# A new written order for the first three batches of a cosine attention with a feed-forward behind it

## The chip, the cores and the metric

The kernel runs on one core of a Trainium2 chip. The metric is the device time of one execution in microseconds (us); the number quoted for a kernel is the median of its runs.

## What is computed

```python
q, k, v: (8, 12, 448, 64) float32      # batch, heads, sequence, head size
q_n = q / (norm(q, axis=-1) + 1e-06);  k_n = k / (norm(k, axis=-1) + 1e-06)
scores = q_n @ k_n.transpose(0, 1, 3, 2) / tau            # tau = 0.1
attn = exp(scores - max);  attn = attn / (sum(attn) + 1e-09)
x = (attn @ v).transpose(0, 2, 1, 3).reshape(8 * 448, 768)
h = x @ w_in                                              # (768, 2048)
out = maximum(0.01 * h, h) @ w_out                        # (2048, 768), float32
```

## The kernel before

Everything is written as **steps**. `ORDER` (lines 16 to 98) is one long string of 1,261 steps; lines 727 to 729 go through it and call, for each step, a small function that emits that step's instructions. Each engine gets its instructions in the order in which the steps stand, and runs them in that order; waits between engines follow from the tiles that a step reads and writes. So moving a step moves it on its own engine only, but it also changes which buffer or PSUM bank it gets. A step is a name and numbers: `k.3.1` is `scores(3, 1)`.

- A **slot** is one pair of heads: slots 0 to 5 are batch 0, slots 6 to 11 batch 1. From slot 12 on the data is laid out otherwise: a **unit** takes two pairs, an even slot holds its queries and the odd one behind it its keys (slots 12 and 13 are unit 0, slots 14 and 15 unit 1).
- Loads. `lq.s` loads a slot through SP's DMA queue (L219, L238 to L244, L230); slots 0 to 5 are loaded by lines 651 to 659, ahead of all steps. `lv.j` loads v for four heads (L256), `lr.b.lo.hi` the last 64 rows of v of batch b, one DMA for each of heads lo to hi (L264). `wi.0` to `wi.3` load w_in in four parts (L182): parts 0 and 1 are its columns 0 to 1023, parts 2 and 3 the others, and each part holds every other block of 128 rows, so a product with m up to 7 needs parts 0 and 1, one with m from 8 up parts 2 and 3. `wo.0`, `wo.1.0.8`, `wo.1.8` load w_out (L188), `lg.g` the v of a group of units (L282). All but `lq` are issued by GpSimd (POOL), on a queue of its own.
- Holds. `hr` (L707) and `hp.s` (L704) are tiny copies on GpSimd that wait for slot 0's data and for slot s's normalised tile, and so hold back what stands behind them on POOL. `hs.s` (L701) does the same for SP's queue.
- Norms. `sq.s.0` squares the queries of a slot, `sq.s.1` the keys, on GpSimd (L306; L300 from slot 12); `qf` and `sa` do that for slots 0 and 1 on ScalarE (ACT). `su` and `uf` sum the squares on VectorE (DVE; L319, L330), `ro` takes the root on ACT as Ln and Exp (L336, L337), `no` makes the reciprocal and multiplies on DVE (L342, L343, L359).
- Turning. `tp.s` transposes a slot on TensorE (PE) into a PSUM bank (L374); `tc` copies it out on DVE (L390), `ta` on ACT. For slot 0 this is done in two parts. From slot 12 on `tt` transposes on DVE (L400) and `td.u` spreads unit u by six DMAs on SP's queue (L409).
- Attention. `k.s.i` is the scores of key tile i (0 to 2; tile 3 is the remaining 64 keys of two slots) into two PSUM banks (L427), `x.s.i` its exponential on ACT (L438). For four heads j, `to.j` sums the exponentials (16 matmuls), `pr.j.0` and `pr.j.1` multiply them with v (16 matmuls each, L450; the last four of the 16 are those with the remaining keys), `ln.j` and `in.j` make the inverse on ACT (L462, L466), `sc.j.e` scales into `xT` on DVE (L478). For units the same is `q`, `y`, `g`, `gl`, `gi`, `gx` (L492, L500, L538, L546, L550, L564).
- Feed-forward. `f.c.m` is six matmuls of w_in's block m with chunk c of tokens (L588); with further numbers only those of the named blocks of 128 rows, so that it can begin before all heads are there. `r` is the leaky ReLU on ACT (L602). `s.c.t.lo.hi` is 16 matmuls with w_out (L624), `o` copies the result out on DVE and writes it (L640, L648).
- `w.n` is n matmuls on a constant tile: work without a use, put where PE would stand idle (L695). `tg` (L709): before it, pairs of banks are dealt from banks 0 to 3 and single banks from 4 to 7; behind it all eight are one pool. A bank is dealt in the order of the steps to the one given back longest ago.

Loaded slots from 6 on have four buffers, so `lq.10` waits for `no.6`, and so on. `hT` has one buffer: the first `r.1.m` waits for the last `s.0`. And each DMA waits for the one eight before it of its kind to land.

Of the kernel before, what the change touches and what calls it, by code (L numbers as in the profile page):

```python
# [26 lines left out]
r.0.0 f.0.1.4.5 r.0.1 f.0.2.4.5 r.0.2 f.0.3.4.5 r.0.3 no.7 lq.11 su.8.0 su.8.1 k.6.0 k.6.1 k.6.2 x.6.0 x.6.1
x.6.2 f.0.4 r.0.4 f.0.5 r.0.5 tp.7 tc.7 ro.8 no.8 hp.8 sq.10.0 sq.10.1 lv.4 wo.1.0.8 su.9.0 su.9.1 f.0.6 r.0.6
f.0.7 r.0.7 k.7.0 k.7.1 x.7.0 x.7.1 f.0.8 r.0.8 tp.8 tc.8 ro.9 no.9 hs.9 lq.12 su.10.0 su.10.1 f.0.9 r.0.9
f.0.10 r.0.10 k.7.2 k.7.3 x.7.2 x.7.3 f.0.11 r.0.11 tp.9 tc.9 ro.10 no.10 hp.10 sq.11.0 sq.11.1 wo.1.8 lv.5  # L30
# [6 lines left out]
su.15 s.0.1.384.768 o.0.1.384.768 ro.15 to.5 ln.5 in.5 pr.5.0 pr.5.1 sc.5.0 sc.5.1 s.0.2.384.768 o.0.2.384.768
no.15 tt.15 td.1 lq.19 hp.15 sq.17 su.16 q.0.0 y.0.0 q.0.1 q.0.2 y.0.1 y.0.2 f.1.0 r.1.0 f.1.1 r.1.1 f.1.2
r.1.2 ro.16 f.1.3 r.1.3 no.16 tt.16 lq.20 hp.16 sq.18 su.17 q.0.3 y.0.3 q.0.4 q.0.5 y.0.4 y.0.5 f.1.4 r.1.4
f.1.5 r.1.5 f.1.6 r.1.6 ro.17 f.1.7 r.1.7 no.17 tt.17 td.2 lq.21 hp.17 sq.19 su.18 q.0.6 y.0.6 q.1.0 q.1.1  # L40
y.1.0 y.1.1 f.1.8 r.1.8 f.1.9 r.1.9 f.1.10 r.1.10 ro.18 f.1.11 r.1.11 no.18 tt.18 lq.22 sq.20 su.19 q.1.2
y.1.2 g.0 gl.0 q.1.3 q.1.4 y.1.3 y.1.4 gi.0 f.1.12 r.1.12 f.1.13 r.1.13 f.1.14 r.1.14 ro.19 f.1.15 r.1.15
no.19 q.1.5 y.1.5 g.0.0 gx.0.0 tt.19 td.3 lq.23 hp.19 sq.21 su.20 q.1.6 q.2.0 y.1.6 y.2.0 lg.1 ro.20
s.1.0.0.384 o.1.0.0.384 no.20 tt.20 lq.24 hp.20 sq.22 su.21 q.2.1 y.2.1 q.2.2 q.2.3 y.2.2 y.2.3 s.1.0.384.768
o.1.0.384.768 ro.21 s.1.1.0.384 o.1.1.0.384 no.21 tt.21 td.4 lq.25 sq.23 su.22 q.2.4 y.2.4 q.2.5 q.2.6 y.2.5
y.2.6 s.1.1.384.768 o.1.1.384.768 ro.22 s.1.2.0.384 o.1.2.0.384 no.22 tt.22 lq.26 hp.22 sq.24 su.23 q.3.0
y.3.0 g.1 gl.1 q.3.1 q.3.2 y.3.1 y.3.2 gi.1 ro.23 s.1.2.384.768 o.1.2.384.768 no.23 q.3.3 y.3.3 g.1.0 gx.1.0
tt.23 td.5 lq.27 hp.23 sq.25 su.24 q.3.4 q.3.5 y.3.4 y.3.5 ro.24 s.1.3.0.384 o.1.3.0.384 q.3.6 y.3.6 g.1.1
gx.1.1 q.4.0 q.4.1 y.4.0 y.4.1 lg.2 s.1.3.384.768 o.1.3.384.768 no.24 tt.24 lq.28 sq.26 su.25 q.4.2 y.4.2
q.4.3 q.4.4 y.4.3 y.4.4 f.2.0 r.2.0 f.2.1 r.2.1 f.2.2 r.2.2 f.2.3 r.2.3 f.2.4 r.2.4 ro.25 f.2.5 r.2.5 no.25  # L50
tt.25 td.6 lq.29 hp.25 sq.27 su.26 q.4.5 y.4.5 q.4.6 q.5.0 y.4.6 y.5.0 f.2.6 r.2.6 f.2.7 r.2.7 f.2.8 r.2.8
# [713 lines left out]
```

## Time and profile before

| | us |
|---|---|
| median of three runs (414.4 to 415.75) | 415.35 |
| the profiled execution: its time, its span | 415.95, 414.0 |
| TensorE busy, of the span | 403.3 |
| VectorE, ScalarE, GpSimd busy | 261.5, 247.3, 113.6 |
| mean granted clock of TensorE | 1.000 |
| `w.20` ends | 7.50 |
| first score product (`k.0.0`), first exponential (`x.0.0`) | 9.62, 10.03 |
| end of the multiply of slot 3 (`no.3`) | 20.73 |
| w_in parts 0, 1 have landed | 24.2, 30.5 |
| first product with w_in (`f.0.0.0.2`) | 31.40 |
| transposes of slot 6 (`tp.6`) | 36.92 |
| w_in part 3 and w_out's first half have landed | 42.0, 53.4 |
| `pr.3.0`, the first product with batch 1's v | 59.62 |
| first scores of unit 0 and unit 1 (`q.0.0`, `q.1.0`) | 81.60, 93.75 |

In the timeline views a row is a run of like instructions on one engine: its start in the span, how long it took from first start to last end, engine, line, operation, tiles, how many, and in brackets how long the engine had been idle before it and what ended that. An end on PE is that of the last matmul with its way through the array; the next matmul starts some 0.15 us before it.

### The profile page before, as it was taken

How to read it: one execution, taken by the hardware profiler on the slowest of the kernel's cores; microseconds unless marked ns; L12 is line 12 of the kernel's file. 1: busy time of each engine (PE TensorE's matmuls, PEld its weight loads, DVE VectorE, ACT ScalarE, POOL GpSimd, SP SyncE). 2: the span in 40 equal slices, each digit the busy share in tenths (PEclk: the TensorE clock that was granted, in tenths of full speed). 3: DMA queues.
4: the chain of work that ended last, by engine and by line, in shares of the span. 5: the costliest groups of instructions: out<-in, count | busy, mean ns of one | idle time of the engine just before them, and what ended most of it. 6: DMA issues, size and time to landing. Idle time of an engine off the chain costs nothing.

```text
span 414.0 us, 11078 instructions
## 1 busy us (share of the span) xinstructions
PE 403.3 (97%) x4662; PEld 211.0 (51%) x4679; DVE 261.5 (63%) x424; ACT 247.3 (60%) x431; POOL 113.6 (27%) x125
## 2 busy tenths in 40 slices
...
GB/s 184 234 203 220 218 222 201 257 166 114 62 212 193 209 112 56 181 232 98 96 136 159 178 154 165 79 206 83 2 90 78 87 40 0 2 70 7 2 114 76
DMA packets 41976, 53.81 MB, mean 130 GB/s; under 512 B 12486, under 2 KB 32326, under 8 KB 41926
## 3 DMA queue, kind: packets, MB, share of 16 engines
...
q10 hardware_dynamic: 688, 0.30, 0.2%
q14 instruction: 14, 0.11, 0.1%
...
## 4 chain that ended last, share of the span: by engine, by line
PE 83%; DMA 6%; DVE 3%; issue 2%; ACT 2%; POOL 2%; SPq 1%; POOLq 0%; DVEq 0%
PE ps L624 33%; PE ps L588 32%; PE ps L538 7%; PE ps L492 6%; DMA qk_h<-in_k_dram 3%; PE ps L450 2%; DMA vq<-in_v_dram 2%; DVE qn L359 1%; DVE ss L319 1%; ACT pe L438 1%; DMA xT<-in_q_dram 1%; PE ps L427 1%; POOL sq L306 1%; SPq L409 1%; PE ps L524 1%
## 5 line engine op out<-in xcount | busy, mean ns | idle before, releaser
L624 PE MATMUL ps<-w_out_sb,hT 128*128 128x384 bf16 (+1 forms) x912 | 151.7, 324 | 0.0
L588 PE MATMUL ps<-xT,w_in_sb 128*128 128x384 bf16 (+1 forms) x753 | 150.3, 352 | 1.0 <-issue 0.3
L500 ACT ACTIVATE pe<-ps 128x896 bf16<-128x896 f32 x126 | 109.2, 917 | 46.8 <-PE ps L492 46.6
L624 PEld LDWEIGHTS <-hT 128*128 128x128 bf16 x912 | 86.4, 98 | 64.4 <-issue 10.7
L588 PEld LDWEIGHTS <-w_in_sb 128*128 128x128 bf16 x768 | 72.9, 98 | 73.5 <-issue 9.0
L602 ACT ACTIVATE hT<-ps 128x384 bf16<-128x384 f32 (+1 forms) x128 | 65.0, 552 | 62.3 <-PE ps L588 44.1
L300 POOL TENSOR_TENSOR sq<-qk_h 128x896 f32<-128x896 f32 x36 | 62.5, 1740 | 60.1 <-DMA qk_h<-in_k_dram 33.6
L640 DVE COPY osb<-ps 128x384 f32<-128x384 f32 (+1 forms) x57 | 30.7, 544 | 76.5 <-PE ps L624 72.9
L349 DVE TENSOR_TENSOR qn<-qk_h,r 128x896 bf16<-128x896 f32 x36 | 42.7, 1186 | 1.6 <-DVE r L343 0.4
L316 DVE TENSOR_REDUCE ss<-sq 128x14 f32<-128x910 f32 x36 | 38.1, 1062 | 1.1 <-POOL sq L300 1.1
L438 ACT ACTIVATE pe<-ps 128x896 bf16<-128x896 f32 x42 | 36.0, 917 | 3.2 <-PE ps L427 3.1
L492 PE MATMUL ps<-qkT 64*32 64x448 bf16 x1008 | 36.0, 352 | 0.3 <-DVE osb L640 0.3
L508 DVE TENSOR_TENSOR shared<-shared,pe 128x896 f32<-128x896 f32 x30 | 35.6, 1218 | 0.3
L564 DVE TENSOR_TENSOR xT<-ps,rb 128x448 bf16<-128x448 f32 x32 | 18.3, 614 | 20.3 <-ACT rb L550 12.4
L400 DVE STREAM_TRANSPOSE tt<-qn 128x448 f32<-128x448 f32 x36 | 29.3, 817 | 0.7
L704 POOL CAST seen<-qn 128x1 f32<-128x1 bf16 x21 | 3.9, 185 | 92.0 <-DVE qn L349 86.0
L342 DVE TENSOR_REDUCE r<-norms 128x14 f32<-128x28 f32 x48 | 8.4, 176 | 31.1 <-ACT norms L337 30.8
L538 PE MATMUL ps<-pe,vq 64*32 64x448 bf16 x1008 | 27.0, 349 | 0.0
L492 PEld LDWEIGHTS <-qkT 64*32 64x32 bf16 x1008 | 12.6, 91 | 19.2 <-issue 15.0
L336 ACT ACTIVATE ss<-ss 128x14 f32<-128x14 f32 x48 | 10.3, 215 | 18.3 <-DVE ss L316 17.2
L282 POOL DMA_DIRECT2D vq<-in_v_dram x20 | 12.7, 639 | 26.6 <-PE ps L492 26.6
L538 PEld LDWEIGHTS <-vq 64*32 64x32 bf16 x1008 | 14.6, 93 | 8.6 <-issue 0.6
...
## 6 DMA issues: line engine op xcount, KB each, us to landing
...
```

What stands on the lines that cost most here:

```text
L300: gp.tensor_tensor(sq[:, :, :D], x, x, op=ALU.mult)
L316: nc.vector.tensor_reduce(o, sqs[s], axis=AX.X, op=ALU.add)
L349: nc.vector.tensor_tensor(qn[s].rearrange("p m d e -> p m e d"), raw[s].rearrange(f"p ({t[1:-1]} d) -> p m e d", e=n, d=D), r.rearrange(f" ...
L438: nc.scalar.activation(out=dst, in_=sc[:, :, :S], func=AF.Exp, scale=inv_tau)
L492: nc.tensor.matmul(out=sc[32 * strip : 32 * strip + 32, a, :S], lhsT=x[rows, c0 : c0 + 32], rhs=x[rows, 0:S], start=True, stop=True,)
L500: nc.scalar.activation(out=pq[u, i], in_=sc[:, :, :S], func=AF.Exp, scale=inv_tau)
L508: eng.tensor_tensor(whole[u], pq[u, 0] if i == 1 else whole[u], pq[u, i], op=ALU.add)
L538: nc.tensor.matmul(out=po[32 * strip : 32 * strip + 32, w, :S], lhsT=weights, rhs=pq[us[x if two else 0], i][rows, a, :], start=(i == 0), ...
L588: nc.tensor.matmul(out=pm[:, :n], lhsT=w_in_sb[:, kt, m * 128 : (m + 1) * 128], rhs=xT[c // 2][:, kt, c0 : c0 + n], start=(done + i == 0), ...
L602: nc.scalar.activation(out=hT[c][:, m, :n], in_=pm[:, :n], func=AF.Prelu, alpha=0.01)
L624: nc.tensor.matmul(out=po2[:, : hi - lo], lhsT=hT[c][:, m, ts * 128 : (ts + 1) * 128], rhs=w_out_sb[:, m, lo:hi], start=(m == 0), stop=(m ...
L640: nc.vector.tensor_copy(out=o[:, lo:hi], in_=bank(("s", c, ts, lo))[:, : hi - lo])
```

## The change

Only `ORDER` changes, and in it only the first 487 steps; the other 774 stand as they were. The same steps are there, each once, `w` steps included: nothing is added or left out. By engine, as the order of each engine's instructions shows:

- **PE**: `tp.0.4.7` before `tp.0.0.4`; key tiles in other sequences (`k.1.2 k.1.1 k.1.3 k.1.0`, `k.2.2 k.2.0 k.2.1`, ...); `pr.0.1` before `tp.3` and `to.0`; the first w_in products before `k.5.3` and `k.5.1`; whole blocks `f.0.m` in the order 5, 6, 4, 7, 13, 15, 11, 9, 8, 10, 14, 12 instead of 4 to 15; `tp.9` before `tp.8`; `k.6.0` and the `k.9` tiles later or earlier; `pr.3` before `tp.11`; `to.5`, `pr.5` before the second halves of `s.0`; `q.0.x` before the last of them.
- **ACT**: `ro.1` before `ta.0.0.4`; `in.0` after `x.3.3`; `ro.9` before `ro.8`; `ln.5` before `ln.4`; `ro.15` before `ro.14`.
- **DVE**: `su.1` in front of `tc.0.4.7` as before, in the other sequence; `su.2.0` before `no.1`; `no.3` before `su.4`; `no.9` before `su.8.0` and `no.8`; `no.12 no.13` before `tt.12 tt.13`; `no.15` long before `no.14`.
- **POOL**: `hr` from the first place to behind `sq.5.0`, so `sq.2` stands in front of `lr.0.0.2`; keys squared before queries in slots 3, 4, 6, 8, 9; `wi.0 wi.1` one behind the other, `wi.3` before `wi.2`; `lr.1.0.4` behind `sq.9`; `lv.5` and `lv.4` behind `wo.1.0.8`; `sq.12` before `wo.1.8`; `sq.15` before `sq.14`; `lg.0` behind `sq.20`.
- **SP**: `lq.8` before `hs.3`; `lq.15` and `td.0` before `lq.14`; `lq.18 lq.19 lq.20` before `td.1`; `lq.22 lq.23 lq.24` before `td.3`.
- `tg` moves from behind the first w_in products to ahead of `k.0.0`.

```diff
-w.20 qf.0.0.3 uf.0.0.3 qf.1.0.3 uf.1.0.3 qf.0.3.4 uf.0.3.4 ro.0 hr lr.0.0.2 sa.1.1 sa.1.0 no.0 su.1.1 lq.6
-sq.2.0 sq.2.1 lv.0 tp.0.0.4 ta.0.0.4 tp.0.4.7 su.1.0 tc.0.4.7 w.3 ro.1 k.0.0 x.0.0 k.0.1 x.0.1 w.2 no.1 su.2.0
-su.2.1 lq.7 hp.1 sq.3.0 sq.3.1 lr.0.2.4 wi.0 k.0.2 x.0.2 ro.2 tp.1 tc.1 w.2 k.1.0 x.1.0 k.1.1 x.1.1 w.2 no.2
-su.3.0 sq.4.0 sq.4.1 lv.1 wi.1 k.1.2 x.1.2 w.2 tp.2 tc.2 k.1.3 x.1.3 su.3.1 ro.3 w.2 k.2.0 x.2.0 k.2.1 x.2.1
-to.0 ln.0 in.0 su.4.0 no.3 hs.3 lq.8 sq.5.0 sq.5.1 lv.2 su.4.1 k.2.2 x.2.2 tp.3 tc.3 pr.0.0 ro.4 k.3.0 x.3.0
-k.3.1 x.3.1 pr.0.1 w.2 su.5.0 no.4 lq.9 su.5.1 sc.0.0 hp.4 sq.6.0 sq.6.1 wi.2 k.3.2 x.3.2 w.2 ro.5 tp.4 tc.4
-k.3.3 x.3.3 w.2 k.4.0 x.4.0 k.4.1 x.4.1 to.1 ln.1 in.1 no.5 sc.0.1 hp.5 sq.7.0 sq.7.1 wi.3 k.4.2 x.4.2 tp.5
-tc.5 pr.1.0 k.5.0 x.5.0 k.5.1 x.5.1 pr.1.1 sc.1.0 sc.1.1 su.6.0 su.6.1 su.7.0 su.7.1 wo.0 sq.8.0 sq.8.1 lv.3
-lr.1.0.4 k.5.2 x.5.2 f.0.0.0.2 f.0.1.0.2 k.5.3 x.5.3 f.0.0.1 f.0.1.1 f.0.0.3 f.0.1.3 tg ro.6 to.2 ln.2 in.2
...
-lq.13 f.0.12 r.0.12 k.8.0 k.8.1 k.8.2 x.8.0 x.8.1 x.8.2 f.0.13 r.0.13 tp.10 tc.10 su.11.0 su.11.1 f.0.14
-r.0.14 f.0.15 r.0.15 ro.11 k.9.0 k.9.1 k.9.2 x.9.0 x.9.1 x.9.2 no.11 hp.11 sq.12 sq.13 hs.11 lq.14 s.0.0.0.384
-o.0.0.0.384 su.12 tp.11 tc.11 to.3 ln.3 in.3 pr.3.0 pr.3.1 sc.3.0 sc.3.1 ro.12 k.10.0 k.10.1 x.10.0 x.10.1
...
+qf.0.0.3 qf.1.0.3 uf.0.0.3 qf.0.3.4 uf.1.0.3 uf.0.3.4 w.20 ro.0 no.0 sa.1.1 sq.2.0 tp.0.4.7 sq.2.1 sa.1.0
+su.1.0 su.1.1 tp.0.0.4 lr.0.0.2 lq.6 lv.0 sq.3.1 ro.1 ta.0.0.4 tc.0.4.7 sq.3.0 w.2 tg w.2 lr.0.2.4 k.0.0
+su.2.0 lv.1 sq.4.1 no.1 x.0.0 su.2.1 k.0.2 k.0.1 sq.4.0 w.2 tp.1 tc.1 x.0.1 w.3 x.0.2 ro.2 wi.0 su.3.1 wi.1
+lq.7 sq.5.0 no.2 k.1.2 w.2 k.1.1 k.1.3 k.1.0 su.3.0 x.1.2 x.1.1 x.1.0 ro.3 w.2 tp.2 tc.2 w.2 x.1.3 w.2 no.3
+k.2.2 k.2.0 k.2.1 x.2.2 x.2.1 pr.0.1 su.4.1 x.2.0 su.4.0 ro.4 tp.3 tc.3 hr hp.1 sq.5.1 su.5.0 to.0 k.3.0 ln.0
+k.3.1 k.3.2 no.4 lq.8 hp.4 lv.2 su.5.1 x.3.0 x.3.2 pr.0.0 x.3.1 w.2 tp.4 tc.4 ro.5 k.3.3 no.5 k.4.1 x.3.3 in.0
+x.4.1 wi.3 to.1 hp.5 pr.1.0 tp.5 ln.1 k.4.2 sq.6.1 sc.0.1 sc.0.0 in.1 tc.5 sc.1.0 k.4.0 pr.1.1 sq.6.0 x.4.2
+k.5.2 sc.1.1 k.5.0 x.4.0 wi.2 f.0.0.0.2 f.0.1.0.2 sq.7.0 su.6.0 x.5.2 k.5.3 x.5.0 su.6.1 ro.6 k.5.1 sq.7.1
+wo.0 x.5.1 su.7.0 x.5.3 f.0.1.3 f.0.1.1 f.0.0.3 f.0.0.1 f.0.3.0.1.2.3 f.0.2.0.1.2.3 lv.3 sq.8.1 hs.3 su.7.1
+no.6 sq.8.0 to.2 ro.7 lq.9 ln.2 pr.2.1 sq.9.1 in.2 sc.2.1 pr.2.0 tp.6 sc.2.0 f.0.5 f.0.2.4.5 r.0.2 tc.6 sq.9.0
...
+lq.12 lv.4 x.9.0 ro.11 x.8.0 s.0.0.0.384 x.8.1 no.11 lq.13 o.0.0.0.384 k.10.1 k.9.3 k.8.2 x.8.2 sq.12 pr.3.0
+pr.3.1 tp.11 tc.11 x.9.3 in.3 x.10.1 s.0.1.0.384 wo.1.8 sq.13 hp.8 su.12 sc.3.0 sc.3.1 k.11.1 k.11.2 k.11.0
+su.13 o.0.1.0.384 ro.12 x.11.1 hp.10 x.11.0 ro.13 hs.11 s.0.2.0.384 x.11.2 k.10.2 no.12 x.10.2 k.11.3 k.10.0
+no.13 tt.12 tt.13 x.10.0 to.4 x.11.3 lq.15 pr.4.1 pr.4.0 to.5 pr.5.1 pr.5.0 ln.5 hp.13 s.0.0.384.768 hp.11
+sq.15 ln.4 in.4 td.0 su.15 lq.14 sq.14 hp.12 s.0.1.384.768 o.0.2.0.384 lq.16 in.5 q.0.2 ro.15 sc.4.1 lq.17
+sc.5.1 no.15 sc.4.0 o.0.0.384.768 sq.16 sc.5.0 o.0.1.384.768 y.0.2 hp.15 q.0.1 q.0.0 su.14 tt.15 f.1.9
+s.0.2.384.768 y.0.0 y.0.1 r.1.9 f.1.13 ro.14 sq.17 su.16 o.0.2.384.768 q.0.3 q.0.5 lq.18 q.0.4 ro.16 y.0.3
+no.14 lq.19 f.1.0 f.1.5 sq.19 y.0.5 f.1.4 f.1.12 f.1.10 no.16 r.1.4 r.1.12 r.1.5 su.17 tt.14 f.1.6 f.1.15
+r.1.10 ro.17 tt.16 no.17 r.1.0 tt.17 su.19 f.1.1 lq.20 td.1 td.2 lq.21 hp.16 y.0.4 r.1.13 r.1.6 q.1.0 q.1.1
...
```

More of the change, by code (lines that the diff above doesn't have):

```diff
@@ L27 @@
[L27 to L30, printed above, removed]
-lq.13 f.0.12 r.0.12 k.8.0 k.8.1 k.8.2 x.8.0 x.8.1 x.8.2 f.0.13 r.0.13 tp.10 tc.10 su.11.0 su.11.1 f.0.14
@@ L37 @@
[L37 to L51, printed above, removed]
```

48 lines of the change are left out of this document (30 added, 18 removed).

## The prediction

> **What bounds the kernel now.** I read the busy shares first, then stretches of the span, then the timeline of each engine in the first stretch, then the DMA queues. TensorE is busy 403.3 of 414.0 us, at a granted clock of 1.00 throughout. The change adds and removes no matmul, so it can only move TensorE's idle time. Where that lies, the stretches tell (span, then busy time of PE, weight loads, DVE, ACT, POOL, clock, DMA share, GB/s):
>
> ```profile
> 0.00:31.40 31.40, 25.16 (x220) 9.86 (x222) 23.87 (x60) 24.32 (x42) 21.89 (x34) 1.00 1.02 207
> 31.40:80.00 48.60, 48.54 (x507) 26.28 (x506) 38.63 (x71) 33.77 (x68) 24.80 (x29) 1.00 1.18 221
> 350.00:414.00 64.00, 60.80 (x463) 34.13 (x464) 9.89 (x19) 12.36 (x23) 0.00 (x0) 1.00 0.13 44
> ```
>
> 6.24 us are idle before the first product with w_in at 31.40 and next to none from there to 350; the last 3.2 lie in steps that don't change. So the change wins or loses in the opening, and what it wins must survive to 130 us, where the old order resumes. The DMA share above 1 from 0 to 80 us says that the DMA engines are full there too. In the opening TensorE waits for short chains (idle time and its releaser in brackets):
>
> ```profile
> 9.62 0.55 PE L427 MATMUL ps<-qkT 64*128 64x448 bf16 x4 [0.34 <-DVE qkT L390]
> ...
> 20.32 0.81 PE L374 MATMUL ps<-id,qn 128*128 128x128 bf16 x7 [1.23 <-DVE qn L359]
> ...
> 31.40 0.82 PE L588 MATMUL ps<-xT,w_in_sb 128*128 128x384 bf16 x4
> ...
> 36.92 0.55 PE L374 MATMUL ps<-id,qn 128*128 128x128 bf16 x7
> ```
>
> The largest, 1.23 us, is `tp.3` behind `no.3`.
>
> **Part by part.** *1. The first copies.* ScalarE's timeline:
>
> ```profile
> 8.29 0.56 ACT L390 COPY qkT<-ps 128x512 bf16<-128x512 bf16 x1
> 9.34 0.22 ACT L336 ACTIVATE ss<-ss 128x14 f32<-128x14 f32 x1 [0.48 <-DVE ss L319]
> ...
> 10.03 2.54 ACT L438 ACTIVATE pe<-ps 128x896 bf16<-128x896 f32 x3 [0.23 <-PE ps L427]
> ```
>
> The copy `ta.0.0.4` used idle time ahead of `ro.1`. Now it stands behind it: `su.1.0` follows `sa.1.0` (end 8.38) and with `su.1.1` ends at 9.6, `ro.1` (0.46) at 10.1, the copy (0.56) at 10.6. `k.0.0` goes from 9.62 to 10.6, `x.0.0` from 10.03 to 11.0. Price: **1.0 us** at the head of ACT's chain. That `tp.0.4.7` goes first, and so waits until 8.28 instead of 7.82, lies under that wait.
>
> *2. Slot 3 is normalised earlier.* `su.4.0`, which waited for POOL until 18.45, stands behind `no.3` now. `hr` no longer stops POOL at the start, and `sq.3.1` needn't wait for the remaining rows, so `sq.3` ends at 14.1 instead of 15.36. `x.1` runs from 13.8 to 16.3 (three at a stride of 0.81), `su.3.0` ends at 16.2, `ro.3` at 16.7; `no.3` (1.65) starts at 16.75 instead of 19.09. What may stretch it is in VectorE's rows:
>
> ```profile
> 13.58 2.20 DVE L359 TENSOR_TENSOR qn<-xT,r 128x512 bf16<-128x512 f32 x2
> ...
> 19.57 1.16 DVE L359 TENSOR_TENSOR qn<-xT,r 128x512 bf16<-128x512 f32 x2
> ```
>
> The first row is `no.2`, beside GpSimd's squares at 13.09 to 15.36; the same two multiplies otherwise take 1.16. In the new order `no.2` is clear of squares and `no.3` lies beside `sq.4.0`, so `no.3` costs 0 to 1.04 more; I take 0.5 and end it at 18.9 (20.73 before).
>
> *3. The rest of slots 3 to 5.* `pr.0.1` now comes before `tp.3` and needs v. `lr.0.2.4` is issued at 14.0 (two squares and three DMA issues earlier than 15.31 allows) and lands 3.4 to 3.9 later, 17.9 at best; with `lr.0.0.2` and `lv.0` moved behind `sq.2`, up to 19.5. I take 18.8 for its last four matmuls. Then `tp.3` 19.3, `tc.3` 20.7 (21.80), `to.0`, `ln.0`, `x.3` from 21.4 to 23.9 (25.15), because `in.0` is moved behind `x.3.3`. `to.1` can start before `x.3.3` ends, only its last four matmuls need it. `no.5` ends at 25.7 (27.34), `sc.0` at 26.8, `in.1` at 27.2, `sc.1.0` at **27.9** (30.10). `tg` lets a score take any free pair of banks, which ends the waits of 0.2 to 0.35 on exponentials before `k`. The `w` steps fill the same gaps as before and cost nothing as long as they stand in idle time. The first w_in product is at 28.4 instead of 31.40: a head start of 3.0, less `k.5.1` (0.2), which follows later. Of it 2.8 would be left at `tp.6` if the data were there.
>
> *4. w_in and the slot loads.* It isn't all there. `wi.1` is issued at 18.6 (19.98), but `lq.8` no longer waits for `no.3`, so slots 8 and 9 are loaded from 17 and 20.5 instead of 21.6 and 24.4, beside w_in. How the queues share, two stretches show, 18 to 24 and 32 to 40 us:
>
> ```profile
> q0 software_dynamic: 844, 0.92, 105.7%
> q1 hardware_dynamic: 158, 0.05, 3.3%
> ```
>
> ```profile
> q0 software_dynamic: 696, 1.37, 90.3%
> q1 hardware_dynamic: 671, 0.37, 21.9%
> ```
>
> In the first, w_in had the engines alone; in the second, each queue sent as many packets as the other, and 671 packets of the slots took 0.219 x 8 = 1.75 us, 0.0026 each. `wi.1` landed at 30.54, with some 600 slot packets by then. In the new order GpSimd's queue holds 512 + 384 + 384 packets from `lv.1` to the end of `wi.1` (192 KB in 384 B, 768 KB in 2 KB each), so packet for packet some 1,280 slot packets pass: 680 x 0.0026 = 1.8 later; `lv.2`, now behind, takes about 0.7 off. **31.6.** Bounds: 26.2 (18.6 plus the shortest landing, 7.6) and 33.0 (all of both slots ahead). The Trainium skill ("DMA: Bandwidth & Descriptors", Queues, rings and completion order) says that a DMA engine takes turns between queues packet by packet, whatever the packets' size; the two stretches agree. A split by bytes would give `wi.1` at about 30.5.
>
> `f.0.1.3` wants `wi.1` at 29.8 and gets it at 31.6; from there four single matmuls 0.65, `f.0.3` and `f.0.2` 1.3, `to.2` 0.77, `pr.2` 1.53: `tp.6` at **35.9** instead of 36.92, 1.0 us ahead. `x.5.3` (end 32.5) is in time. Then `wi.2`, now last, lands at 42 to 43 (41.99 for the last part before) and is wanted at 43.1 (`f.0.13` stands where `f.0.8` stood, at 44.35, with one `k` less before it).
>
> *5. Batch 1.* The first product with batch 1's v is the next place without slack:
>
> ```profile
> 35.26 2.49 POOL L264 DMA_DIRECT2D shared<-in_v_dram  x4
> ```
>
> ```profile
> DMA to landing us min/median/max: 21.0/22.6/23.2
> ```
>
> These four DMAs are `lr.1.0.4` (GpSimd's timeline, and their landings). The last landed at 59.56, and the last four matmuls of `pr.3.0` began at about 60.2. They queue behind `wo.0` (landed 53.43) and `lv.3`; all that stands ahead of them is the same bytes as before, through engines that are full, and slots 12 and 13 start at about 49.4 instead of 50.09 beside them. So I keep 59.2, with bounds 56.2 (the first of the four) and 60. The new `pr.3.0` has the same work ahead of it (`tp.11` 0.4 less, two `k` more): its last four come at 60.2 - 1.0 = 59.2, just served. A larger head start would end here. `wo.0` is wanted at 55. `lv.4`, now issued at 53.4 behind `wo.1.0.8` (landed 66.0 before, with slot 14's load beside it), should land by 67 and is wanted at 68.
>
> *6. Units.* `td.0` ends on SP at 74 and lands by 76; `q.0.2` wants it at 78.9 - 1.0 = 77.9. But `lq.14` now stands behind `td.0`: issued 74, landed 78.8, `sq.14` 80.5, then on DVE `su.14`, `tt.15`, `su.16`, an output copy, `no.14`, `no.16`, `su.17`, `tt.14` (1.1 + 0.65 + 1.05 + 0.55 + 1.65 + 1.65 + 1.05 + 1.0) to 89.4, `td.1` 3.8 and 2.0 to land: 95.3. `q.1.0` has two `f` more and one `q` less ahead of it than before: 93.75 + 2.7 - 1.0 = 95.4. Just served again. `td.3`, behind `lq.24`, lands 11.2 us after `s.1.0.0.384` ends (copy 0.6, `tt` 1.65, `no.20` 1.65, `lq.24` 1.2, `td.3` 3.75, landing 2.4), and `q.3.0` comes 11.9 after it. I count nothing for both.
>
> *7. The rest:* key tiles and w_in blocks in other sequences, `ln.5` before `ln.4`, `tp.9` before `tp.8`, `lg.0` at 93 for a use at 107. Nothing, since between a score product and the first use of its exponential lie w_in blocks of 0.98 each or whole `s` of 2.6; where that cover is gone, an exponential (0.92) shows.
>
> Sum: 1.0 us won by `tp.6`, kept to the end. On the profiled execution's own time, 415.95 (414.0 span, 1.95 around it), that is 414.95; its time is 0.6 above the median, so in the measure of the runs 415.35 - 1.0, **414.3**.
>
> **The rivals.** *The opening's gain in full.* If `wi.1` lands by 30 and the remainders by 57.5, 2 to 2.7 us stay: 412.6 to 413.4. For it: 27.9 for `sc.1.0` doesn't hang on a DMA. Against it: full DMA engines and four places (`wi.1`, `pr.3.0`, `td.1`, `td.3`) with little slack.
>
> *The late first exponential is not made good: slower.* ACT is busy 24.3 of the first 31.4 us. From `x.0.0` to `x.5.3` it had 21 exponentials at 0.81, four roots at 0.46, two pairs `ln`, `in` at 1.1, 21.0 us, and took 23.5, so 2.5 idle. Now `ro.6` is among them too: 21.5 from 11.0, and with the same idle time `x.5.3` ends at 35.0, the last four matmuls of `to.2` come 1.3 later than before, and so does the end: **416.6**. It decides from 1.0 us of idle time on (11.0 + 21.5 + 1.0 = 33.5, as before); I count 0 to 1, since `ro` and `x` are now seldom late, but fills on newly dealt banks now wait for exponentials as well (`w.2` and `tp.2` for `x.1.2`).
>
> *Unit 1 is late.* Each us that slot 14's chain loses (a load landing after 10 us like slot 10's, two stretched multiplies) is one on TensorE at `q.1.0`: 2 to 4 give 416.3 to 418.3.
>
> **How the numbers follow.** The forecast, 0.3 to 1.9 won: 0.48. The full gain: 0.20. The late exponential: 0.18. Unit 1 late: 0.14. About 0.3% (1.25 us) is what a measurement of this kernel can tell from no change. The forecast puts 0.18 beyond that and 0.30 within; the full gain is faster; of the late exponential 0.04 is within, the rest and unit 1 slower: faster 0.38, same 0.34, slower 0.28. Range: from the full gain's 412.6 to the late exponential's 416.6; unit 1 is left out. The forecast's own range is 413.4 to 415.1.
>
> **What would show it.** `k.0.0` at 10.6; `no.3` ending near 18.9 and `sc.1.0` near 27.9; an idle stretch of some 1.8 us on PE before `f.0.1.3`, released by the w_in DMA; `tp.6` at 35.9; no gap at `pr.3.0` and `q.1.0`. Wrong: `x.5.3` after 33.5, a gap over 1 us at `pr.3.0` or `q.1.0`, or `wi.1` before 30.

## The result and the profile after

The changed kernel takes **417.27 us** (median of 14 runs, 415.33 to 420.19) where the kernel before takes 415.33 on the same chip (14 runs, 414.40 to 416.08): ratio **1.0051, 95% interval 1.0036 to 1.0067**. The forecast was 414.3, faster, with 416.6 as the upper end. It came out slower, and outside the range.

The profiled execution of the changed kernel took 417.69 us, with a span of 415.9. Its stretches (columns as before: span, then busy time of PE, weight loads, DVE, ACT, POOL, clock, DMA share, GB/s):

```profile
0.00:29.85 29.85, 25.77 (x217) 10.51 (x219) 24.29 (x60) 22.04 (x40) 18.83 (x31) 1.00 1.00 217
29.85:80.00 50.15, 47.99 (x526) 26.20 (x524) 39.16 (x70) 34.67 (x68) 23.69 (x28) 1.00 1.03 186
80.00:130.00 50.00, 48.46 (x564) 24.18 (x560) 34.50 (x53) 34.30 (x60) 20.89 (x21) 1.00 0.65 160
350.00:415.90 65.90, 62.69 (x474) 35.20 (x475) 9.90 (x19) 14.11 (x27) 0.00 (x0) 1.00 0.12 43
```

Idle time of PE is span less busy time. Ahead of the first product with w_in it fell from 6.24 to 4.08 us. From there to 80 us it rose from 0.06 to 2.16, and between 80 and 130 us it is 1.54 (0.21 before, by the same view). The end is as it was: 3.21. So the opening won and the two stretches behind it lost more. Idle time makes the opening look better than it is: the matmuls without a use of `w.20` happened to take 7.28 us here and 5.85 before, and that counts as busy. PE's timeline shows where (start, time, then idle time and releaser in brackets):

```profile
10.55 0.74 PE L427 MATMUL ps<-qkT 64*128 64x448 bf16 x6 [0.36 <-ACT qkT L390]
...
20.56 0.56 PE L374 MATMUL ps<-id,qn 128*128 128x128 bf16 x7
...
29.85 0.82 PE L588 MATMUL ps<-xT,w_in_sb 128*128 128x384 bf16 x4
...
32.02 2.12 PE L588 MATMUL ps<-xT,w_in_sb 128*128 128x384 bf16 x12 [0.65 <-DMA w_in_sb<-in_moe_w_in_dram]
...
36.46 0.56 PE L374 MATMUL ps<-id,qn 128*128 128x128 bf16 x7
...
57.21 0.34 PE L374 MATMUL ps<-id,qn 128*128 128x128 bf16 x3 [1.49 <-DVE qn L359]
...
87.01 0.38 PE L492 MATMUL ps<-qkT 64*32 64x448 bf16 x8 [0.90 <-DVE osb L640]
```

From the top: `k.0.0`; `tp.3`, whose wait of 1.23 us is gone; the first w_in product, 1.55 earlier than before; `f.0.1.3` behind w_in's second part; `tp.6`, 0.46 ahead of the kernel before; and then two waits that the prediction didn't have, 1.49 us at `tp.10` and 0.90 at `q.0.4`. With those, 0.46 ahead becomes, for equal work done, 1.1 behind at the first `s.0` and about 1.6 behind at `q.1.0`.

**The wait at `tp.10`.** VectorE's rows of the four normalises `no.2`, `no.3`, `no.6` and `no.10` (their two multiplies), and further down the sum `su.16` and the output copy `o.0.2.384.768`:

```profile
14.51 2.02 DVE L359 TENSOR_TENSOR qn<-xT,r 128x512 bf16<-128x512 f32 x2
...
18.15 1.16 DVE L359 TENSOR_TENSOR qn<-xT,r 128x512 bf16<-128x512 f32 x2
...
32.80 3.18 DVE L359 TENSOR_TENSOR qn<-qk_h,r 128x512 bf16<-128x512 f32 x2
...
53.98 3.17 DVE L359 TENSOR_TENSOR qn<-qk_h,r 128x512 bf16<-128x512 f32 x2
...
85.39 1.10 DVE L316 TENSOR_REDUCE ss<-sq 128x14 f32<-128x910 f32 x1 [1.60 <-POOL sq L300]
86.40 0.55 DVE L640 COPY osb<-ps 128x384 f32<-128x384 f32 x1
```

GpSimd's rows for the same times: v's load `lv.4`, slot 12's squares `sq.12`, and later slot 14's squares `sq.14`:

```profile
54.21 0.81 POOL L256 DMA_DIRECT2D shared<-in_v_dram  x1 [1.07 <-DMA w_out_sb<-in_moe_w_out_dram]
55.03 1.69 POOL L300 TENSOR_TENSOR sq<-qk_h 128x896 f32<-128x896 f32 x1
...
80.42 1.68 POOL L300 TENSOR_TENSOR sq<-qk_h 128x896 f32<-128x896 f32 x1 [7.59 <-DMA qk_h<-in_q_dram]
```

The two multiplies of a normalise take 1.16 us alone and 3.17 beside `sq.12`: 2.01 more, a little over the whole 1.69 of the square. The single records of the trace say the same: the second multiply of `no.10` runs from 54.59 to 57.15, and `sq.12` from 55.03 to 56.73; the multiply ends 0.42 after the square. In the kernel before `no.10` had 1.65 us in all, 1.16 of it the multiplies, since slot 11's squares stood behind the hold on `no.10` and slot 12's behind the hold on `no.11`. VectorE's row of `no.10` there, and GpSimd's of the two holds:

```profile
51.63 1.16 DVE L359 TENSOR_TENSOR qn<-qk_h,r 128x512 bf16<-128x512 f32 x2
```

```profile
52.92 0.18 POOL L704 CAST seen<-qn 128x1 f32<-128x1 bf16 x1 [1.25 <-DVE qn L359]
...
57.83 0.19 POOL L704 CAST seen<-qn 128x1 f32<-128x1 bf16 x1 [1.29 <-DVE qn L359]
```

The change moves both holds (`hp.10`, `hp.11`) behind slot 12's squares and loads slot 12 earlier (issued at 45.87, not 50.09). `no.6` is stretched as far, by the squares of slots 8 and 9, but `tp.6` didn't wait for it.

GpSimd's row of `lv.4`, further up, tells what set the collision. GpSimd stood still for 1.07 us, until w_out's first part had landed (53.92), because `lv.4` is the eighth DMA behind `wo.0` of its kind. `sq.12` stands behind `lv.4`, so the landing of w_out decides when it runs.

The Trainium skill ("SBUF — State Buffer", 🔬 SBUF: two separate sides) states that VectorE with two SBUF inputs and GpSimd share one pair of ports, that it is an exclusive lock for a whole instruction, and that the other one fully blocks. The 3.17 against 1.16 agrees. By its record the multiply started 0.44 us ahead of the square and was yet the one that waited, so which of the two had the pair first can't be read off the records. GpSimd was issuing `lv.4` when it started (54.21 to 55.01). That issue alone isn't what stretched it: in experiment 17 below, the same two multiplies stood beside the same issue (54.01 to 54.81), with the square held back, and took 1.16.

`no.2` is another matter. Its first multiply ran from 14.51 to 16.06, 1.55 us instead of 0.69, with no square beside it. GpSimd's rows there are squares, two issues of v's last rows, the issue of v's second tile, and squares again:

```profile
12.04 2.23 POOL L306 TENSOR_TENSOR sq<-xT 128x384 f32<-128x384 f32 x2
14.22 1.29 POOL L264 DMA_DIRECT2D shared<-in_v_dram  x2
15.51 0.79 POOL L256 DMA_DIRECT2D shared<-in_v_dram  x1
16.31 1.89 POOL L306 TENSOR_TENSOR sq<-xT 128x384 f32<-128x384 f32 x2
```

The same multiply took 1.55 to 1.56 us, again beside these issues alone, in the profiled executions of experiments 1, 2, 6, 9, 10, 13 and 14. `no.3`, beside the issues of w_in (18.16 to 19.73), ran at full speed. So an issue can stretch a multiply as well; when it does, the runs don't tell.

**The wait at `q.0.4`.** `lq.14`, now behind `td.0`, was issued at 75.99 (58.41 before), `sq.14` began at 80.42, and `sq.16` behind it at 83.67. VectorE stood 1.60 us for `sq.16` at `su.16`, and behind that sum came the copy `o.0.2.384.768` at 86.40, which gives back the bank that `q.0.4` needs.

The queue view of the stretch from 18 to 24 us (packets, MB, share of 16 engines), which the prediction showed for the kernel before:

```profile
q0 software_dynamic: 974, 0.75, 84.0%
q1 hardware_dynamic: 1054, 0.55, 34.7%
```

The slots' queue moved 1,054 packets beside GpSimd's 974 (158 beside 844 before). From 32 to 40 us it is the other way, 83 beside 987 (671 beside 696 before). The slots now load early, beside w_in.

### The profile page after: what moved, and what is told of

It is laid out like the page before. It is cut to its first block, busy times and chain, and to the rows that moved or that the text cites. A ratio compares the mean times of both kernels' runs of the same rounds, so it can differ in the third digit from the quotient of the medians.

```text
span 415.9 us, 11073 instructions
## 1 busy us (share of the span) xinstructions
PE 403.8 (97%) x4662; PEld 212.3 (51%) x4679; DVE 264.5 (64%) x424; ACT 245.8 (59%) x431; POOL 115.9 (28%) x125
## 3 DMA queue, kind: packets, MB, share of 16 engines
q0 software_dynamic: 15504, 11.80, 19.5%
## 4 chain that ended last, share of the span: by engine, by line
PE 85%; DMA 7%; DVE 3%; POOL 1%; SPq 1%; issue 1%; ACT 1%; POOLq 0%; DVEq 0%
PE ps L588 34%; PE ps L624 33%; PE ps L538 8%; PE ps L492 7%; DMA w_in_sb<-in_moe_w_in_dram 3%; PE ps L450 2%; DMA qk_h<-in_q_dram 1%; DVE qn L359 1%; DMA xT<-in_k_dram 1%; PE ps L427 1%; DMA qkT<-tt 1%; PE ps L374 1%; DVE ss L319 1%; PE ps L524 1%; SPq L409 0%
## 5 line engine op out<-in xcount | busy, mean ns | idle before, releaser
L602 ACT ACTIVATE hT<-ps 128x384 bf16<-128x384 f32 (+1 forms) x128 | 64.0, 550 | 64.5 <-PE ps L588 44.7
L300 POOL TENSOR_TENSOR sq<-qk_h 128x896 f32<-128x896 f32 x36 | 63.6, 1771 | 76.6 <-DMA qk_h<-in_k_dram 34.1
L349 DVE TENSOR_TENSOR qn<-qk_h,r 128x896 bf16<-128x896 f32 x36 | 44.8, 1245 | 1.4
L508 DVE TENSOR_TENSOR shared<-shared,pe 128x896 f32<-128x896 f32 x30 | 34.1, 1168 | 0.3
L564 DVE TENSOR_TENSOR xT<-ps,rb 128x448 bf16<-128x448 f32 x32 | 18.3, 616 | 20.4 <-ACT rb L550 12.4
L704 POOL CAST seen<-qn 128x1 f32<-128x1 bf16 x21 | 5.5, 260 | 75.8 <-DVE qn L349 72.3
```

The lines of the kernel that those rows point to most:

```text
L300: gp.tensor_tensor(sq[:, :, :D], x, x, op=ALU.mult)
L349: nc.vector.tensor_tensor(qn[s].rearrange("p m d e -> p m e d"), raw[s].rearrange(f"p ({t[1:-1]} d) -> p m e d", e=n, d=D), r.rearrange(f" ...
L508: eng.tensor_tensor(whole[u], pq[u, 0] if i == 1 else whole[u], pq[u, i], op=ALU.add)
L602: nc.scalar.activation(out=hT[c][:, m, :n], in_=pm[:, :n], func=AF.Prelu, alpha=0.01)
```

## Experiments

Ratios are to the kernel before on the same chip, whose medians there were 415.37 (experiments 1 to 4), 415.02 (5 to 8), 415.36 (9 to 12), 415.46 (13 to 15) and 415.42 (16 and 17). All kernels differ only in `ORDER`. A ratio is not the quotient of the two medians: that of experiment 3 is 0.9974, while its medians give 0.9994.

**1. The hold ahead of slot 12's squares** (the changed kernel with one step moved):

```diff
-x.8.2 sq.12
+x.8.2 hp.10 sq.12
...
-x.11.1 hp.10 x.11.0
+x.11.1 x.11.0
```

> The changed kernel with one step moved: hp.10, GpSimd's wait for slot 10's normalised tile, back in front of the squares of slot 12. Theory A (what was lost is the time that VectorE's normalise stands still beside GpSimd's squares; in the changed kernel no.10 took 3.65 us instead of 1.65 and tp.10 waited 1.49 for it): no.10 takes 1.65 again, the gap before tp.10 goes, 1.5 to 2 us come back, about 415.5. Rival B (the loss is slot 14's chain, whose place on SP's queue is unchanged): no.10 is short, but TensorE waits at q.0.4 for as much more, about 417. Rival C (the late first exponential): 417, and x.5.3 ends as late as before.

Measured: 416.64 us, ratio 1.0018 (0.9988 to 1.0048): some 0.6 us came back, not 1.5 to 2. `no.10` took 1.65 us, and `tp.10` waited for nothing. The squares of slot 13 now met `no.11` (3.34 us), which showed as 0.55 at `pr.3.1`. The wait at `q.0.4` stayed, at 0.47.

**2. Slot 14's load ahead of `td.0`** (the changed kernel with one step moved):

```diff
-x.11.3 lq.15 pr.4.1
+x.11.3 lq.15 lq.14 pr.4.1
...
-su.15 lq.14 sq.14
+su.15 sq.14
```

> The changed kernel with lq.14, the load of slot 14, moved from behind td.0 to directly behind lq.15 on SP's queue, some 12 us earlier. Theory B: su.14 and su.16 no longer hold the output copy that q.0.4's banks wait for, the gap of 0.90 before q.0.4 goes, and 0.9 to 1.3 us come back: 416.2. Theory A alone: the gap before tp.10 stays at 1.5, and the time at 417, since what is saved at q.0.4 is lost at td.1 or td.3.

Measured: 416.18, ratio 1.0012 (0.9989 to 1.0036). `su.14` ran at 80.50 instead of 82.13, the copy at 84.72 instead of 86.40, and the wait at `q.0.4` was gone; the one at `tp.10` stayed (1.33).

**3. Both.**

> Both moves together: hp.10 in front of the squares of slot 12 and lq.14 behind lq.15. If A and B are both right and add up, 2.4 to 3 us come back: 414.3 to 415, at or below the kernel before. If only one is right, the same time as that one alone.

Measured: 415.11, ratio 0.9974 (0.9944 to 1.0004). Both waits were gone, and the loss with them, though 0.55 us at `pr.3.1` remained as in experiment 1. By the ratio this is as near as any version came to beating the kernel before, but the interval holds 1 and the medians are 0.26 us apart. What is left to explain is the opening: `f.0.1.3` waited 1.36 us for w_in here.

**4. The hold behind the squares, in the kernel before:**

```diff
-no.10 hp.10 sq.11.0 sq.11.1 wo.1.8
+no.10 sq.11.0 sq.11.1 hp.10 wo.1.8
```

> The kernel before with one step moved: hp.10 from in front of slot 11's squares to behind them, so that these may run beside no.10. Theory A: no.10 takes 2.5 to 3.7 us instead of 1.65, tp.10 waits 0.8 to 1.8 us, and the kernel takes 416.2 to 417. If the squares beside the normalise are not what stretches it: no.10 stays at 1.65 and the time at 415.3.

Measured: 416.46, ratio 1.0005 (0.9977 to 1.0033). This test missed: slot 11 had only landed at 52.50, so the squares met no normalise (`no.10` 1.65). In its profiled execution (418.45) GpSimd stood for 4 us ahead of `lv.5`:

```profile
59.50 0.75 POOL L256 DMA_DIRECT2D shared<-in_v_dram  x1 [4.04 <-DVE osb L640]
```

`lv.5` is the eighth DMA behind `lv.3`, which landed at 58.96 here and at 54.57 in the kernel before. The releaser that the row names had to do with it by time only: the list of waits of that instruction has a DMA and a PE semaphore, none of VectorE. `hp.11` and `sq.12` stood behind `lv.5`, and PE waited 2.02 us at `k.10.1`. So the landing of a DMA eight issues back cost 2 us in an order that is the kernel before's but for one step.

**5. w_in ahead of v's second tile** (with both moves of experiment 3, as all that follow but 7 and 17):

```diff
-lr.0.2.4 k.0.0 su.2.0 lv.1
+lr.0.2.4 wi.0 wi.1 k.0.0 su.2.0 lv.1
```

> Both moves of before (GpSimd's hold ahead of slot 12's squares, slot 14's key load ahead of td.0), and now w_in's first two parts issued ahead of v's second tile (wi.0 and wi.1 directly behind lr.0.2.4, so at about 15.5 us instead of 18.1 and 18.9). Theory (after the two moves the opening is bound by w_in's second part): wi.1 lands near 29.5 instead of 32.0, the 1.36 us gap on PE before f.0.1.3 goes, tp.6 comes near 35.4 (36.47), where no.6, which ended at 35.3, takes over; time about 414.1 (415.1 with the two moves alone). Rival (the loads of slots 4 and 5 and v's second tile only change places with w_in): slot 4's or 5's key load lands later, a gap as long opens at tp.3 to tp.5 or at pr.1.0, time 415 or more.

Measured: 422.14, ratio 1.0157 (1.0132 to 1.0181). `wi.1` landed at 28.9, but `lv.1`, issued 1.35 us later than in experiment 3, landed at 31.2 instead of 21.2. PE's waits between 20 and 60 us:

```profile
PE ps L450 <- DMA shared<-in_v_dram: 4.6, 1, 4.6
```

The rival was right, and by more than it said: `lv.1`'s 192 KB stood behind the 1.5 MB of w_in's two parts, landed after both of them, and came 10 us later than in experiment 3. The wait was at `pr.1.0`.

**6. The first copy ahead of the roots again** (`ta.0.0.4 ro.1` instead of `ro.1 ta.0.0.4`):

> Both moves, and the copy ta.0.0.4 ahead of the roots ro.1 on ScalarE again, as in the kernel before. By part 1 of the prediction the copy behind ro.1 costs 0.9 to 1.0 us at k.0.0 and that is on the path: k.0.0 at 9.6 instead of 10.4, and the whole opening with it, time about 414.2. By the rival (w_in's second part binds the opening, whatever comes ahead of it): k.0.0 and the slots come 0.5 to 0.9 earlier, the gap before f.0.1.3 grows by the same, and the time stays within 0.4 us of the 415.1 of the two moves alone.

Measured: 414.88, ratio 0.9992 (0.9978 to 1.0007). `k.0.0` came at 9.58 instead of 10.36, and the gap before `f.0.1.3` stayed (0.94). The time shows no gain against experiment 3, as the rival has it. The profiled execution doesn't quite fit it, since `tp.6` came 0.92 us earlier than there (35.55), with w_in's second part 0.92 earlier too (31.07). So what the copy is worth stays open.

**7. A normalise beside squares, in the kernel before:**

```diff
-no.11 hp.11 sq.12 sq.13
+no.11 sq.12 hp.11 sq.13
```

> The kernel before with one step moved: hp.11, GpSimd's hold on slot 11's normalised tile, goes from ahead of slot 12's squares to behind them, so that these squares begin as soon as GpSimd has issued lv.5 (56.5 us) and run beside no.11 (56.05 to 57.70 before). Theory A (a normalise beside these squares takes 2 us longer): no.11 takes 2.7 to 3.7 us instead of 1.65, tp.11 waits for it 0.7 to 1.5 us, and the time is about 416.1 to 416.9 (415.35 before). Rival (the stretch is at most the 1.04 us of the prediction, and tp.11 has cover): no.11 at most 2.7, a wait of at most 0.4, time within 0.5 us of before.

Measured: 415.45, ratio 1.0016 (0.9997 to 1.0034). VectorE's and GpSimd's rows:

```profile
55.62 2.64 DVE L359 TENSOR_TENSOR qn<-qk_h,r 128x512 bf16<-128x512 f32 x2
```

```profile
56.14 1.71 POOL L300 TENSOR_TENSOR sq<-qk_h 128x896 f32<-128x896 f32 x1 [0.69 <-DMA qk_h<-in_q_dram]
```

The multiplies went from 1.16 to 2.64, only a hold being moved: the stretch is shown. Its price was less than expected, a wait of 0.48 at `tp.11`, since PE had work until 57.84.

**8. Experiments 5 and 6 and a new hold `hp.6` behind `no.6`:**

> The two moves, w_in's first two parts ahead of v's second tile, the copy ta.0.0.4 ahead of ro.1, and one more hold on GpSimd behind no.6, so that slot 8's squares no longer run beside it. Theory (w_in's second part and then no.6 bind what is left of the opening): no gap before f.0.1.3, no.6 at 1.65 us instead of 3.67, tp.6 near 34.8, time about 413.4, which is faster than both kernels. Rival (DMA's rate binds the opening): wi.1 still lands after 31.5 or another load is late by as much, tp.6 after 36, and the time stays at 415.

Measured: 421.65, ratio 1.0155 (1.0138 to 1.0173). The wait at `pr.1.0` again (5.35), and slot 8's squares only at 40.6. It says no more than experiment 5.

**9. Slot 8's load behind `hs.3` again:**

```diff
-no.4 lq.8 hp.4
+no.4 hs.3 lq.8 hp.4
```

> Both moves, and slot 8's key load behind SP's hold on slot 3's normalised tile (hs.3) again, as in the kernel before: its four transfers are issued from about 20.1 us instead of 16.0. Theory (w_in's second part lands late because slot 8's load takes turns with it from 16 us on): wi.1 lands near 30.5 instead of 31.1 to 32.8, the gap before f.0.1.3 falls from the 0.9 to 1.4 us of the runs with both moves to at most 0.3, tp.6 about 0.6 earlier relative to x.5.3 and the time about 0.6 us under the kernel with both moves alone. Rival (the later load only collides with the same w_in part at another moment): wi.1 still at 31.5 or later and no gain.

Measured: 416.26, ratio 1.0020 (0.9998 to 1.0043). PE's timeline of it: `f.0.1.3`, `tp.6`, `k.7.3`:

```profile
30.50 2.12 PE L588 MATMUL ps<-xT,w_in_sb 128*128 128x384 bf16 x12
...
34.94 0.56 PE L374 MATMUL ps<-id,qn 128*128 128x128 bf16 x7
...
43.35 0.57 PE L427 MATMUL ps<-qkT 64*64 64x448 bf16 x6 [1.34 <-DVE qkT L390]
```

`wi.1` landed at 30.4, the wait before `f.0.1.3` was gone and `tp.6` 1.98 us ahead of the kernel before. The theory of w_in and the slots' packets held for the landing, not for the time. 1.34 us went at `k.7.3`: slot 9's load was now issued at 22.5 (20.4 in experiment 3), beside the later parts of w_in, its last squares came at 40.99 (35.94), and on VectorE the copy `tc.7` stood behind slot 9's sum.

**10. Experiment 9 and `hp.6` behind `no.6`:**

> As the run with slot 8's load behind hs.3, and a new hold on GpSimd behind no.6, ahead of slot 8's squares. Theory A says no.6 takes 1.65 us instead of 3.67 and ends at about 33.8; tp.6 then waits for neither. If tp.6 is bound by no.6 once w_in is in time, it comes 0.5 to 1 us earlier and the time falls by as much; the rival is that tp.6 stands in PE's order behind the f products anyway, so no.6's stretch has cover and the time doesn't change (within 0.3).

Measured: 415.60, ratio 1.0011 (0.9996 to 1.0025). `no.6` took 1.65 us and ended at 32.86; `tp.6` came at 35.19, behind a wait of 0.49 for w_in, and no earlier than in experiment 9, where `no.6` took 2.89. So a stretched normalise, which cost 1.49 us at `tp.10`, costs nothing here. The wait at `k.7.3` stayed, at 1.63.

**11. Experiment 9 and `hp.1` ahead of slot 3's squares:**

```diff
-lv.0 sq.3.1 ro.1 ta.0.0.4 tc.0.4.7 sq.3.0 w.2 tg w.2 lr.0.2.4 k.0.0 su.2.0 lv.1 sq.4.1 no.1
+lv.0 ro.1 ta.0.0.4 tc.0.4.7 w.2 tg w.2 k.0.0 su.2.0 no.1 hp.1 sq.3.1 sq.3.0 lr.0.2.4 lv.1 sq.4.1
```

> As the run with slot 8's load behind hs.3, and GpSimd's hold on slot 1's normalised tile (hp.1) in front of slot 3's squares, as in the kernel before, with v's two loads that stood between the squares behind them. By part 2 of the prediction the squares beside a normalise cost the opening up to 1 us and the earlier squares give it back: no.1 takes 1.65 us instead of 2.3 to 3.3 and tp.1 loses its 0.6 to 1.4 us wait, but slot 3's squares come 0.1 to 0.5 later and v's tiles 1 us later; if lr.0.2.4 or lv.1 bind (pr.0.1, pr.1.0), the wait goes there and w_in's second part lands 1 us later. Theory: no change in time (within 0.4), since w_in's second part binds; rival: 0.6 to 1.0 faster.

Measured: 417.65, ratio 1.0048 (1.0031 to 1.0066). Neither. `no.1` was back at 1.64, but `no.2` met the squares of slot 4, and `tp.2` waited 2.61 us:

```profile
14.12 4.21 DVE L359 TENSOR_TENSOR qn<-xT,r 128x512 bf16<-128x512 f32 x2
```

A hold moves the collision to the next normalise that has none.

**12. All of it:**

> All of it: both moves, slot 8's load behind hs.3, the holds behind no.6 and no.1, and the copy ta.0.0.4 ahead of ro.1. If the opening's waits are separate, each is gone and the time is near 413.2, faster than both kernels by 0.5%. If w_in's second part binds whatever stands ahead of it, the time is that of the run with slot 8's load alone, near 414.5.

Measured: 416.76, ratio 1.0028 (1.0011 to 1.0044). `tp.6` at 35.05, and 1.78 us at `k.7.3`.

**13. Experiment 9 with `tc.7` ahead of the sum `su.9.0`:**

> Both moves, slot 8's load behind hs.3, and on VectorE the copy tc.7 ahead of slot 9's second sum su.9.0, which stood ahead of it and waited for slot 9's load. Theory (the opening's gain was handed to this wait through VectorE's order): the 1.34 us gap at k.7.3 goes, tp.6 stays at 34.9 and the time is about 1.3 us under the run with slot 8's load alone (416.26), near 414.5 to 415. Rival (slot 9's load is what binds): the wait moves to no.9 and tp.9 or to k.9.1, as long as before, and the time doesn't change.

Measured: 414.63, ratio 0.9989 (0.9970 to 1.0008). The wait at `k.7.3` was gone, and the median fell by 1.6 us, though the two intervals overlap. This profiled execution can't show why, since its opening was late (`tp.6` at 36.43, not 34.9) and slot 9's squares were done before `tc.7` had anything to copy. Experiment 14 does: with `tp.6` at 35.17, `tc.7` copied at 40.88 while slot 9's sum waited until 41.97, and `k.7.3` waited for neither. So it was VectorE's order. The profiled execution took 417.62. Its waits on GpSimd between 50 and 66 us, then GpSimd's and VectorE's rows:

```profile
POOL shared L256 <- DMA w_out_sb<-in_moe_w_out_dram: 2.7, 1, 2.7
```

```profile
57.13 1.69 POOL L300 TENSOR_TENSOR sq<-qk_h 128x896 f32<-128x896 f32 x1
...
59.74 1.69 POOL L300 TENSOR_TENSOR sq<-qk_h 128x896 f32<-128x896 f32 x1
```

```profile
57.31 5.15 DVE L359 TENSOR_TENSOR qn<-qk_h,r 128x512 bf16<-128x512 f32 x2
```

w_out's first part landed at 55.9 in this execution (53.7 in experiment 3), so `lv.4` and the squares of slots 12 and 13 came later and met `no.11` with full force: 5.15 us for two multiplies, and 2.70 us of idle time at `pr.3.1`.

**14. Experiment 13, the first copy ahead of `ro.1`, and `hp.6`:**

> As the run with tc.7 ahead of su.9.0, and the copy ta.0.0.4 ahead of ro.1, and the hold behind no.6. If the first copy is on the path once w_in's second part is in time, k.0.0 comes at 9.5 instead of 10.1 to 10.4 and the time is 0.5 to 0.9 lower than without, near 414; if w_in's second part (30.5) binds again, a gap of 0.4 to 0.6 opens before f.0.1.3 and the time is the same within 0.3.

Measured: 414.99, ratio 1.0001 (0.9977 to 1.0025). The profiled execution had a span of 412.5, 1.5 under that of the kernel before, with `k.0.0` at 9.51 and no wait before `f.0.1.3`; the median of 12 shows no gain. The spans flatter it: this execution took 414.55, under its own median, and that of the kernel before 415.95, 0.6 over its own.

**15. Slot 9 loaded, squared and summed ahead of slot 8:**

> Both moves, ta.0.0.4 ahead of ro.1, slot 9's key load behind hs.3 and in front of slot 8's, with GpSimd's squares and VectorE's sums of the two slots in that order too, and tc.7 ahead of su.9.0. Slot 9 is normalised first in this order of steps, slot 8 second. Theory (the order of transfers, not their number, makes a wait): wi.1 lands near 30.5 as with slot 8's load later, slot 9 lands by 33 to 36, neither f.0.1.3 nor k.7.3 nor tp.9 waits more than 0.4, and the time is near 413.8, faster than both kernels. Rival (DMA is full from 18 to 42 us, so that one of the transfers is late whatever the order): wi.2, wi.3 or slot 8 is late by 1 us or more and the time stays at 415.

Measured: 414.66, ratio 0.9992 (0.9970 to 1.0014). Neither `f.0.1.3` nor `k.7.3` nor `tp.9` waited, yet it is no faster than experiment 13: in its profiled execution `no.1` and `no.3` were stretched (3.22 and 2.48 us), with 1.8 us of waits at `tp.1`. PE came to its first w_in product only at 31.23, after w_in's second part had landed (30.63), so that nothing waited there says little.

**16. Experiment 14 with `hp.11` ahead of slot 12's squares:**

> The kernel with both moves, slot 8's load behind hs.3, tc.7 ahead of su.9.0, the hold behind no.6 and ta.0.0.4 ahead of ro.1 (414.99 median, executions from 414.26 to 420.13), and hp.11 ahead of slot 12's squares, so that they run beside neither no.10 nor no.11. Theory A in its wider form (which normalise the squares meet is set by the landing of w_out's first part, and the executions differ by it): no.10 and no.11 take 1.65 us each, no wait at pr.3.1 or tp.11 above 0.4, slot 12's squares begin near 57.5, the median falls to about 414.2 and no execution lies above 417. Rival (the slow executions have another cause): the same spread, with some at 417 to 420, and the median unchanged; or the squares are now late for su.12, with a wait of about 1 us at k.11.0 or q.0.2 and the time 0.5 to 1 higher.

Measured: 414.81, ratio 0.9992 (0.9967 to 1.0017). `no.11` took 1.65, `no.10` 1.76, and nothing waited at `pr.3.1` or `tp.11`. But three of 12 executions still lie above 416.5 (the highest at 417.37), and beside them one of the kernel before took 419.63. So this collision isn't the only source of the scatter.

**17. The changed kernel with `hp.11` ahead of slot 12's squares, nothing else moved:**

```diff
-x.8.2 sq.12
+x.8.2 hp.11 sq.12
```

> The changed kernel with one step moved: hp.11 ahead of slot 12's squares (the earlier run moved hp.10 there: 416.64). Slot 14's late chain stays. Theory A: no.10 and no.11 at 1.65 us, no wait at tp.10, pr.3.1 and tp.11, the wait of 0.5 to 0.9 us at q.0.4 stays, time 416.0 to 416.6 against 417.27 for the changed kernel. Rival (the later squares push su.12 and what follows): a new wait of about 1 us before q.0.0, time 417 or more.

Measured: 415.61, ratio 1.0006 (0.9988 to 1.0024). VectorE's rows of `no.10` and `no.11`:

```profile
53.91 1.16 DVE L359 TENSOR_TENSOR qn<-qk_h,r 128x512 bf16<-128x512 f32 x2
...
57.17 1.16 DVE L359 TENSOR_TENSOR qn<-qk_h,r 128x512 bf16<-128x512 f32 x2
```

Both at full speed, no wait at `tp.10`, and the wait at `q.0.4` still there (0.70). The time is under the 416.0 to 416.6 that were expected. One hold of 0.18 us takes away nearly all of the change's loss: the ratio falls from 1.0051 to 1.0006, 0.45% or 1.9 us.

## Why the prediction was wrong, step by step

- *1, the first copies: right in place, the weight open.* `k.0.0` at 10.55 (10.6), `x.0.0` at 10.95 (11.0). Putting the copy back won no time (experiment 6), but its profiled execution leaves open whether the copy is on the path.
- *2, slot 3: the end roughly right, the stretch wrong in place and size.* `no.3` ended at 19.31 (18.9). It ran free, all but clear of `sq.4.0`, and `no.1` and `no.2` were stretched, by 0.63 and 0.86: `no.2` was clear of squares, as I wrote, but not of v's DMA issues. The price of a normalise beside squares I bounded by 1.04 us, from one row of the kernel before in which the two met only in part, and counted it for `no.3` alone. Beside slot 12's and 13's squares it is about the length of the squares: 1.5 to 2.0 beside one (experiments 7, 1, 2 and the changed kernel), 4.0 beside two (experiment 13).
- *3, slots 3 to 5:* `sc.1.0` started at 28.66 and was put at 27.9, the first w_in product at 29.85 (28.4). v's remainders landed at 20.2, not 17.9 to 19.5, and `no.1` and `no.2` were stretched.
- *4, w_in: right.* `wi.1` landed at 31.98 (31.6; 30.5 by bytes). Moving slot 8's load back brought 30.4 (experiment 9), as a count of packets that take turns has it. The wait was shorter (0.65, not 1.8) because PE came later. `tp.6` was 0.46 ahead, not 1.0; it reached that point at 36.46 (35.9).
- *5, batch 1: right.* The remainders landed at 58.2 (59.2), and `pr.3.0` didn't wait for them. But I put `lv.4` down as a load that is wanted at 68, and didn't ask what stands behind it on GpSimd. It waits for the eighth DMA before it, as the section on the kernel says; `sq.12` stands behind it.
- *6, units: a wait put at nothing cost 0.90.* `sq.14` ended at 82.10 (80.5), as `lq.14` was issued at 75.99 (74). The bank of `q.0.4`, through the output copy behind `su.16`, came in the chain ahead of `td.1` and `q.1.0`; so the rival "Unit 1 is late" had the right load and the wrong place. Experiment 2 took the wait away. The 2.7 us for two blocks more and one key tile less was too much as well: at 1.32 a block and 0.23 a tile, as the rows of the kernel before have them, it is 2.4.
- *7, the rest: "nothing".* **The step that failed is here.** The sum has no term for slot 10's normalise. The holds `hp.10` and `hp.11` moved behind slot 12's squares, and I didn't cost that edit: the list of POOL's moves had named `sq.12` before `wo.1.8` and not the holds, and part 2 allowed for a stretch at `no.3` alone. In place of nothing the runs showed 2.01 us more for `no.10` beside `sq.12` and a wait of 1.49 at `tp.10`. With `hp.11` ahead of the squares again both are gone, and the ratio falls from 1.0051 to 1.0006 (experiment 17). Part 2's bound of 1.04 would have made the term too small in any case.
- *The late exponential.* `x.5.3` ended at 33.72, after the 33.5 that I named as a sign of being wrong, but it cost nothing at `tp.6`.

The sum in the profiled execution: 0.46 won at `tp.6`, 1.49 lost at `tp.10`, 0.90 at `q.0.4`: 1.93 lost, as the spans say (415.9 against 414.0). The agreement is closer than it deserves, since other rows come and go: four pauses of 0.16 with no releaser between 80 and 105 us, which experiment 17 with the same order on PE didn't have, and one of 0.5 at `f.4.9`, which came in some executions and not in others. Their cause isn't known.

What stays open is the scatter of single executions (experiment 16). In experiments 9, 10 and 12 an opening that was 1.7 to 2.0 us ahead at `tp.6` was lost again at `k.7.3` (1.34, 1.63 and 1.78). Experiment 14 was 1.75 ahead and lost nothing there, and why its median shows no gain isn't known. Nor can the loss be divided between the two waits beyond the noise, as experiments 2 and 17 each took away most of it. No version was faster than the kernel before by more than its interval.
